# Top-k attention and a hard-swish feed-forward part: query tiles outermost, 128-token blocks, V as stationary operand, mask on GpSimd

## The chip, the cores and the metric

One core of a Trainium2 chip runs the kernel. Its engines run side by side, each with a queue of its own that it takes in order: TensorE (PE; its weight loads are shown as PEld), VectorE (DVE), ScalarE (ACT), GpSimd (POOL), and SyncE (SP), which here only issues DMAs. The metric is the device time of one execution in microseconds, less is better.

## The reference

Everything is float32, except that the two weight matrices arrive as float64.

```python
# q, k, v: (8 batches, 8 heads, 576 rows, 64)
scores = (q @ k.transpose(0, 1, 3, 2)) / 8
kth = 32nd largest score of each row
scores = where(scores >= kth, scores, -1e9); scores -= max
attn = exp(scores); attn /= attn.sum(-1) + 1e-9
x = (attn @ v), heads side by side          # (4608 tokens, 512)
h = x @ w_in                                # 512 -> 2048
out = (h * clip(h + 3, 0, 6) / 6) @ w_out   # 2048 -> 512
```

## The kernel before

The work is cut into 160 **units**. A pair of heads of one batch has five: four full ones (128 queries of each of the two heads, so two tiles of 128x576 scores) and one "rest" unit (the 64 queries left over of both heads in one tile). Pairs are outermost: all five units of a pair, then the next pair; 20 units make a batch.

For a unit TensorE makes the scores (line 201, contraction over 64 features, the two heads in the two halves of the array's rows), ScalarE copies them to SBUF (L203), and VectorE finds the 32nd largest of each row in four rounds of "eight largest" (L215) and "replace them" (L218). ScalarE takes the exponential (L223, its shift from GpSimd, L221), and VectorE sets to 0 what is below the 32nd largest (L227). TensorE then transposes the weights in blocks of 128x128 (L243, L251), ScalarE copies them back (L244, L252), and ten products per unit give the weighted values (L259): there the transposed weights are the stationary operand, 128x128, and V with a column of ones moves, 65 columns. VectorE divides by the sum (L267 to L270), and one more transpose (L277, copied at L280) puts features on partitions.

The feed-forward part runs over blocks of 512 tokens, one per batch, and one for the left-over rows of all batches. A block has 16 times four products of 512 moving columns (L289), each group followed by a ScalarE relu (L297) and a VectorE gate (L299), then four times 16 products of 512 columns (L307). The program deals a batch's block out in pieces of four products among the units of the next batch; the last batch's block and that of the left-over rows come at the end. Every matrix product in float32 is two instructions in the trace (1152 for 576 products at L307); a transpose is one.

The float64 weights are converted in 64 chunks of 128x256 during the first batch (L101 to L123: a DMA, six VectorE and two GpSimd operations each), through 16 shared buffers. The tile framework's scheduler sets the order on each engine.

Of the kernel before, what the change touches and what calls it, by code (L numbers as in the profile page):

```python
# [15 lines left out]
LOWEST = -3.4028234663852886e38  # L16
EPS = 1.0e-9
# High words of the float64 values that float32 can hold, read as float32: 0x38000000 and
# 0x47efffff. Below the first they become 0.
# [5 lines left out]
def kernel(  # L25
# [16 lines left out]
    NC = J + 1  # L42
    NHP = H // 2
    NFC = FF // P
    TB = JP  # tokens in a block of the feed-forward part
    DE = D + 1
    assert 2 * D == P and 2 * R == P and NHP * P == DM
    assert TB == 512 and DM == 512 and B * R == TB and TOP_K % 8 == 0
# [7 lines left out]
    kqpool = pool("kq", 2)  # L56
    scpool = pool("sc", 3)
    wkpool = pool("wk", 4)
    mpool = pool("m", 3)
    epool = pool("e", 2)  # L60
    etpool = pool("et", 2)
    xpool = pool("x", 2)
    xtpool = pool("xt", 2)
    gpool = pool("g", NFC)
    tpool = pool("t", 2)
    opool = pool("o", 2)
    ps_sc = pool("ps_sc", 1, space=PSUM)
    ps_w = pool("ps_w", 3, space=PSUM)
    ps_acc = pool("ps_acc", 1, space=PSUM)
# [3 lines left out]

    def work():
        return ps_w.tile([P, 512], F32, tag="w", name="w")
# [5 lines left out]
    # A last column of ones gives the sum of the weights next to the weighted values. The last  # L81
    # tile of keys is the last 128 of them: its first half is another tile's, and counts for 0.
    NV = 3
    vring = []
    for i in range(NV):
        t = const([P, 2, NC, DE], f"v{i}")
        nc.gpsimd.memset(t[:], 1.0)
        nc.gpsimd.memset(t[0 : P - R, :, J, :], 0.0)
        vring.append(t)
    w_in = const([P, NHP, FF], "w_in")  # L90
    w_out = const([P, NFC, DM], "w_out")
    x_rest = const([P, NHP, TB], "x_rest")  # left-over rows of all batches: a block of their own

# [1 line left out]

    WC = 256

    def convert(dst, src):
        """dst[P, WC] = src[P, WC], rounded once; src holds float64 bits, low word first."""
        st = gpool.tile([P, 2 * WC], U32, tag="g", name="st")  # L100
# [3 lines left out]
        ta = gpool.tile([P, 2, WC], F32, tag="g", name="ta")  # L104
        sp = gpool.tile([P, 2, WC], F32, tag="g", name="sp")
        t, a, s, p = ta[:, 0, :], ta[:, 1, :], sp[:, 0, :], sp[:, 1, :]
        tu, au, su = t.bitcast(U32), a.bitcast(U32), s.bitcast(U32)
        nc.vector.tensor_scalar(tu, hi, 0x7FFFFFFF, None, ALU.bitwise_and)
        nc.gpsimd.tensor_scalar(t, t, HI_MOST, HI_LEAST, ALU.min, ALU.max)
        # The exponent's top bit stays, the three after it go; the rest moves up by three.  # L110
        nc.vector.tensor_scalar(
            au, tu, 3, 0x3FFFFFFF, ALU.logical_shift_left, ALU.bitwise_and
        )
        nc.vector.scalar_tensor_tensor(
            out=au, in0=tu, scalar=0x40000000, in1=au, op0=ALU.bitwise_and, op1=ALU.bitwise_or
        )
        # The low word counts in units of 2**-52 of the power of two.
        nc.vector.tensor_scalar(su, au, 0x7F800000, None, ALU.bitwise_and)
        nc.vector.scalar_tensor_tensor(
            out=p, in0=lo, scalar=2.0**-52, in1=s, op0=ALU.mult, op1=ALU.mult  # L120
        )
        nc.gpsimd.tensor_tensor(a, a, p, ALU.add)
        nc.vector.scalar_tensor_tensor(  # L123
            out=dst.bitcast(U32), in0=hi, scalar=0x80000000, in1=au,
            op0=ALU.bitwise_and, op1=ALU.bitwise_or,
        )

    def weight_chunks():
        win, wout = moe_w_in.bitcast(U32), moe_w_out.bitcast(U32)
        for f in range(0, FF, WC):  # L130
            for g in range(NHP):
                rows = slice(g * P, (g + 1) * P)
                yield w_in[:, g, f : f + WC], win[rows, 2 * f : 2 * (f + WC)]
        for c in range(NFC):
            for e in range(0, DM, WC):
                rows = slice(c * P, (c + 1) * P)
                yield w_out[:, c, e : e + WC], wout[rows, 2 * e : 2 * (e + WC)]

# [1 line left out]

    class Pair:
        """Two heads of a batch: their loads, and keys and queries with the head dim on partitions."""

        def __init__(self, i):
            self.b, self.hp = divmod(i, NHP)
            self.v = vring[i % NV]

        def load(self):
            h0 = 2 * self.hp
            for name, src in (("kin", k), ("qin", q)):  # L150
                t = ldpool.tile([P, NC, 2, D], F32, tag=name, name=name)
# [9 lines left out]
            for hh in range(2):  # L161
                nc.sync.dma_start(
                    self.v[:, hh, 0:J, 0:D],
                    v[self.b, h0 + hh, 0:JP, :].rearrange("(p j) d -> p j d", j=J),
                )
            nc.sync.dma_start(
                self.v[P - R : P, :, J, 0:D], v[self.b, h0 : h0 + 2, JP:S, :].rearrange("h s d -> s h d")
            )

        def transpose(self):  # L170
            kT = self.kT = kqpool.tile([P, S], F32, tag="kT", name="kT")
            qT = self.qT = kqpool.tile([P, S], F32, tag="qT", name="qT")
            for src, dst in ((self.kin, kT), (self.qin, qT)):
                ps = work()
# [3 lines left out]
                nc.scalar.copy(dst[:, 0:JP], ps[:, 0:JP])  # L178
            ps = work()
# [3 lines left out]
            for i, dst in enumerate((kT, qT)):  # L183
                nc.scalar.copy(dst[:, JP:S], ps[:, i * R : (i + 1) * R])

    class Unit:
        """A tile of queries: 128 of each head of a pair, or the 64 left over of both in one."""
# [6 lines left out]
        def scores(self):  # L194
            pr, nt, q0 = self.pair, self.nt, self.qt * P
            ps = ps_sc.tile([P, 2, 1024], F32, tag="ps", name="ps")
            for s0, s1 in ((0, 512), (512, S)):
                for hh in range(2):
                    d = slice(hh * D, (hh + 1) * D)
                    dst = ps[hh * R : (hh + 1) * R, 0, s0:s1] if self.rest else ps[:, hh, s0:s1]  # L200
                    nc.tensor.matmul(dst, pr.qT[d, q0 : min(q0 + P, S)], pr.kT[d, s0:s1])  # L201
            self.sc = scpool.tile([P, 2, S], F32, tag="sc", name="sc")
            nc.scalar.copy(self.sc[:, 0:nt, :], ps[:, 0:nt, 0:S])  # L203

        def weights(self):
            """exp(scale * (s - max)) where s reaches the row's TOP_K-th largest score, else 0."""
            nt, sc = self.nt, self.sc
            m = mpool.tile([P, 2, TOP_K], F32, tag="m", name="m")
            shift = mpool.tile([P, 2], F32, tag="shift", name="shift")
            e = self.e = epool.tile([P, 2, S], F32, tag="e", name="e")  # L210
            cur = [sc[:, t, :] for t in range(nt)]
            for r in range(TOP_K // 8):
                for t in range(nt):
                    m8 = m[:, t, 8 * r : 8 * r + 8]
                    nc.vector.max(m8, cur[t])  # L215
                    if r < TOP_K // 8 - 1:
                        wk = wkpool.tile([P, S], F32, tag="wk", name="wk")
                        nc.vector.match_replace(wk[:], m8, cur[t], LOWEST)  # L218
                        cur[t] = wk[:]
                if r == 0:  # L220
                    nc.gpsimd.tensor_scalar_mul(shift[:, 0:nt], m[:, 0:nt, 0], -scale)  # L221
                    for t in range(nt):
                        nc.scalar.activation(  # L223
                            e[:, t, :], sc[:, t, :], AF.Exp, bias=shift[:, t : t + 1], scale=scale
                        )
            for t in range(nt):
                nc.vector.scalar_tensor_tensor(  # L227
                    out=e[:, t, :],
                    in0=sc[:, t, :],
                    scalar=m[:, t, TOP_K - 1 : TOP_K],  # L230
                    in1=e[:, t, :],
                    op0=ALU.is_ge,
                    op1=ALU.mult,
                )

        def values(self, dst):
            """Weighted values over the sum of the weights, with features on partitions, to dst."""
            pr, nt, e = self.pair, self.nt, self.e
# [182 lines left out]
```

## Time and profile before

| | us |
|---|---|
| median of three runs | 2309.13 (2308.7 to 2310.08) |
| span of the profiled execution, first to last instruction | 2307.1 |
| TensorE matmuls busy | 2060.9 (89%) |
| VectorE busy | 1874.4 (81%) |
| ScalarE busy | 760.6 (33%) |
| GpSimd busy | 120.0 (5%) |

The span is that of one execution; the runs' time lies 2.0 us above it. A busy share is a mean over the span, in which three stretches differ: the first batch with the weights' conversion up to some 440 us, the seven batches up to 2076 us, and the last two feed-forward blocks. The clock that TensorE was granted is one of two levels, 1.2 and 2.4 GHz; the windows' column gives its mean as a share of 2.4 GHz.

### The profile page before, as it was taken

What the parts mean: (1) busy time and instruction counts of PE and PEld (TensorE: products, weight loads), DVE (VectorE), ACT (ScalarE), POOL (GpSimd) and SP (SyncE); (2) the same over time, 40 slices, a digit from 0 to 9 for tenths busy, and PEclk for the clock granted to TensorE, in tenths of its full rate; (3) what the DMA queues carried; (4) which work ended last, traced back from release to release, by engine and by line L of the source; (5) the groups of instructions that cost most, each with busy time, mean ns of one, the idle gap of its engine ahead of it and who ended that gap; (6) DMA issues with size and microseconds to landing.
All of it is one profiled execution on the core that took longest, in us unless ns stands there. A gap on an engine that the chain in (4) does not pass through costs nothing.

```text
span 2307.1 us, 25080 instructions
## 1 busy us (share of the span) xinstructions
PE 2060.9 (89%) x8704; PEld 1170.3 (51%) x8704; DVE 1874.4 (81%) x4177; ACT 760.6 (33%) x1365; POOL 120.0 (5%) x300
## 2 busy tenths in 40 slices
PE   7566662799999999999899989998999999999998
PEld 4444441456555655555455545565555555654443
DVE  7999988689998998989898989988998989881010
ACT  3222220234343433433334333333334333431020
POOL 1222212000000000000000000000000000000000
PEclk9765556799999998999999999999999999999999
DMA  3021211000100000000000100000001000000000
GB/s 98 28 75 42 71 42 46 11 16 22 29 16 16 25 25 16 16 21 25 21 8 22 32 11 16 19 23 25 16 11 31 25 11 6 10 10 0 14 5 18
DMA packets 129790, 56.15 MB, mean 24 GB/s; under 512 B 116864, under 2 KB 116864, under 8 KB 129664
## 3 DMA queue, kind: packets, MB, share of 16 engines
q1 hardware_dynamic: 129664, 54.55, 8.8%
q8 instruction: 69, 1.13, 0.2%
q14 instruction: 57, 0.47, 0.1%
HBM read 45.09 MB, written 9.44 MB: 24 GB/s over the span
## 4 chain that ended last, share of the span: by engine, by line
PE 72%; DVE 7%; ACT 2%; issue 1%; DVEq 0%; POOL 0%; ACTq 0%
PE w L289 22%; PE acc L307 20%; PE w L259 12%; PE ps L201 10%; PE w L251 5%; DVE m L215 3%; DVE wk L218 2%; PE w L243 1%; PE w L277 1%; DVE e L227 1%; ACT sc L203 1%; PE w L177 1%; PE w L182 0%; DVE x L270 0%; DVE den L267 0%
## 5 line engine op out<-in xcount | busy, mean ns | idle before, releaser
L215 DVE MAX8 m<-wk 128x8 f32<-128x576 f32 x864 | 624.3, 747 | 0.8
L307 PE MATMUL acc<-w_out,g 128*128 128x512 f32 x1152 | 548.4, 607 | 2.1 <-ACT o L317 2.1
L201 PE MATMUL ps<-kT,qT 64*128 64x64 f32 (+3 forms) x1280 | 399.0, 501 | 113.2 <-ACT sc L203 113.0
L289 PE MATMUL w<-xT,w_in 128*128 128x512 f32 x1024 | 476.7, 619 | 0.0
L259 PEld LDWEIGHTS w<-v,eT 128*128 128x128 f32 (+1 forms) x3200 | 374.8, 195 | 104.8 <-ACT eT L252 55.3
L218 DVE MATCH_REPLACE8 wk<-m,wk 128x576 f32<-128x576 f32 x576 | 425.3, 741 | 0.3 <-issue 0.3
L259 PE MATMUL w<-v,eT 128*128 128x65 f32 (+1 forms) x3200 | 390.7, 279 | 3.4 <-ACT eT L252 3.3
L203 ACT COPY sc<-ps 128x1152 f32<-128x1152 f32 (+1 forms) x160 | 163.7, 1023 | 481.8 <-PE ps L201 259.4
L289 PEld LDWEIGHTS w<-xT,w_in 128*128 128x128 f32 x1024 | 200.1, 201 | 228.6 <-issue 227.1
L307 PEld LDWEIGHTS acc<-w_out,g 128*128 128x128 f32 x1152 | 200.7, 190 | 181.0 <-issue 165.3
L201 PEld LDWEIGHTS ps<-kT,qT 64*128 64x128 f32 (+1 forms) x1280 | 144.2, 192 | 262.1 <-ACT sc L203 149.3
L223 ACT ACTIVATE e<-sc,shift 128x576 f32<-128x576 f32 x288 | 214.2, 776 | 130.4 <-POOL shift L221 130.0
L297 ACT ACTIVATE t<-w,three 128x512 f32<-128x512 f32 x144 | 99.0, 687 | 474.2 <-PE w L289 417.4
L299 DVE SCALAR_TENSOR_TENSOR g<-t,w 128x512 f32<-128x512 f32 x144 | 97.9, 680 | 191.7 <-ACT t L297 191.6
L227 DVE SCALAR_TENSOR_TENSOR e<-sc,m,e 128x576 f32<-128x576 f32 x288 | 228.0, 807 | 8.6 <-ACT e L223 8.2
L215 DVE MAX8 m<-sc 128x8 f32<-128x576 f32 x288 | 212.2, 745 | 18.1 <-ACT sc L203 17.7
L218 DVE MATCH_REPLACE8 wk<-m,sc 128x576 f32<-128x576 f32 x288 | 212.8, 740 | 0.0
L251 PE MATMUL w<-ident,e 128*128 128x128 f32 x1152 | 179.6, 294 | 2.2 <-ACT xT L280 0.7
L252 ACT COPY eT<-w 128x512 f32<-128x512 f32 x288 | 162.6, 591 | 46.0 <-PE w L251 41.6
L251 PEld LDWEIGHTS w<-ident,e 128*128 128x128 f32 x1152 | 144.2, 152 | 34.2 <-ACT eT L252 21.2
L221 POOL TENSOR_SCALAR shift<-m 128x2 f32<-128x2 f32 (+1 forms) x160 | 38.2, 239 | 1662.0 <-DVE m L215 1095.0
L267 DVE TENSOR_SCALAR den<-w 128x2 f32<-128x2 f32 (+1 forms) x160 | 24.6, 154 | 120.4 <-PE w L259 120.3
(45 smaller groups left out, 885.1 us busy)
## 6 DMA issues: line engine op xcount, KB each, us to landing
kin<-in_k_dram SPq DMA_DIRECT2D x64, 128.0 KB, 2.7
qin<-in_q_dram SPq DMA_DIRECT2D x64, 128.0 KB, 2.9
v<-in_v_dram SPq DMA_DIRECT2D x64, 128.0 KB, 2.7
st<-in_moe_w_in_dram SPq DMA_DIRECT2D x32, 256.0 KB, 3.7
st<-in_moe_w_out_dram SPq DMA_DIRECT2D x32, 256.0 KB, 3.3
out_dram<-o SPq DMA_DIRECT2D x32, 256.0 KB, 2.3
kin<-in_k_dram SPq DMA_DIRECT2D x32, 32.0 KB, 2.4
qin<-in_q_dram SPq DMA_DIRECT2D x32, 32.0 KB, 2.5
```

Of the source, the lines that this page charges most:

```text
L201: nc.tensor.matmul(dst, pr.qT[d, q0 : min(q0 + P, S)], pr.kT[d, s0:s1])
L203: nc.scalar.copy(self.sc[:, 0:nt, :], ps[:, 0:nt, 0:S])
L215: nc.vector.max(m8, cur[t])
L218: nc.vector.match_replace(wk[:], m8, cur[t], LOWEST)
L223: nc.scalar.activation(e[:, t, :], sc[:, t, :], AF.Exp, bias=shift[:, t : t + 1], scale=scale)
L227: nc.vector.scalar_tensor_tensor(out=e[:, t, :], in0=sc[:, t, :], scalar=m[:, t, TOP_K - 1 : TOP_K], in1=e[:, t, :], op0=ALU.is_ge, op1=AL ...
L251: nc.tensor.transpose(ps[:, cs], e[:, t, cs], ident[:])
L252: nc.scalar.copy(eT[:, t, 0:J, :], ps[:, 0:JP].rearrange("p (c q) -> p c q", c=J))
L259: nc.tensor.matmul(o[:, hh, :], eT[:, t, c, q0 : q0 + ql], pr.v[:, hh, c, :], start=(c == 0), stop=(c == J),)
L289: nc.tensor.matmul(h[:], w_in[:, i, f * P : (f + 1) * P], xT[:, i, :], start=(i == 0), stop=(i == NHP - 1),)
L297: nc.scalar.activation(t[:], h[:], AF.Relu, bias=three[:], scale=1.0)
L307: nc.tensor.matmul(acc[:], gs[f][:, ts * P : (ts + 1) * P], w_out[:, f, :], start=(f == 0), stop=(f == NFC - 1),)
```

## The change

Within a batch the query tile is now the outer loop and the four pairs the inner one: four units (one tile of 128 queries, all eight heads) complete a block of 128 tokens, whose feed-forward part can follow at once. There are 36 such blocks: four per batch, and one for the left-over rows of every two batches. A block is eight pieces: four of 16 products with 128 moving columns (four chunks of the hidden layer in one PSUM bank, one relu and one gate on 128x512 for all four), and four of four products with 512 moving columns. In the values' products V is the stationary operand (64 columns; the output of one head goes to partitions 0 to 63, of the other to 64 to 127) and the transposed weights move, 128 columns. The scores of both heads lie side by side; the last 64 keys of both heads are one product over all 128 rows.

The mask is made on GpSimd (compare and multiply by -3e38, add to the scores, both before the exponential); the exponential gives the sum of the weights, and ScalarE multiplies the weights by its reciprocal before they are transposed. The transpose of x and the division on VectorE are gone. Weights are converted in 32 chunks of 128x512 through two load buffers, with other operations. The order on each engine is now the order of the code. Cut to its core (the new kernel's lines):

```diff
+    scpool = pool("sc", 4)
+    stpool = pool("st", 2)
+    cvpool = pool("cv", 2)
+    opool = pool("o", 1)
     ps_sc = pool("ps_sc", 1, space=PSUM)
+    ps_tr = pool("ps_tr", 2, space=PSUM)
+    ps_w = pool("ps_w", 2, space=PSUM)
+    ctx.enter_context(tc.manual_schedule())
...
         nc.sync.dma_start(st[:], src)
...
+        nc.scalar.activation(f, lo, AF.Copy, scale=2.0**-52)
+        nc.scalar.activation(a, hi.bitcast(F32), AF.Abs)
+        nc.gpsimd.tensor_scalar(a, a, HI_MOST, HI_LEAST, ALU.min, ALU.max)
...
+        nc.vector.tensor_scalar(au, au, 0x40000000, None, ALU.bitwise_xor)
+        nc.gpsimd.tensor_tensor(f, f, s, ALU.mult)
+        nc.gpsimd.tensor_tensor(a, a, f, ALU.add)
...
+                nc.tensor.matmul(ps[:, 0:JP], pr.qT[h0, qs], pr.kT[h0, :])
+                nc.tensor.matmul(ps[:, S + R : 1024], pr.qT[h1, qs], pr.kT[h1, 0 : 1024 - S - R])
+                nc.tensor.matmul(ps[:, 1024:W2], pr.qT[h1, qs], pr.kT[h1, 1024 - S - R : JP])
+                nc.tensor.matmul(ps[:, JP : S + R], pr.qT[:, qs], pr.kr[:].rearrange("p h r -> p (h r)"))
+                nc.scalar.copy(sc[:], ps[:, 0:W2])
...
+                nc.gpsimd.tensor_scalar(
+                    self.wk[:, t, :], self.row[t], self.m[:, t, TOP_K - 1 : TOP_K], DROP,
+                    ALU.is_lt, ALU.mult,
+                )
...
+                nc.scalar.activation(
+                    self.row[t], self.row[t], AF.Copy, scale=self.den[:, t : t + 1]
+                )
...
+                    nc.tensor.matmul(
+                        dst[hh * D : (hh + 1) * D, :],
+                        pr.vm[:, hh, c, :] if c < J else pr.vr[:, hh, :],
+                        rhs,
...
+            g = gpool.tile([P, 512], F32, tag="g", name="g")
+            nc.scalar.activation(g[:], h[:], AF.Relu, bias=three[:], scale=1.0)
...
+        if u:
+            u.begin()
+            u.top(0)
+        run_gate()
+        if n >= FF_FROM:
+            piece()
+        if u:
+            u.top(1)
+        if 2 <= n < NU + 2:
+            units[n - 2].weights()
...
+        if u:
+            u.top(2)
+        run_gate()
+        if n >= FF_FROM and (two or n % 4 == 3):
+            piece()
...
+        if n >= 2 and n < NU + 2 and (n - 2) % 2 == 1:
+            values(n - 2)
+        if u:
+            u.top(3)
+        if chunks:
+            convert_some(3)
+        if n >= FF_FROM and two and n % 4 == 3:
+            run_gate()
+            piece()
+        if u:
+            u.mask()
+        if 1 <= n < NU + 1:
+            units[n - 1].exp()
```

In iteration n VectorE thus works on unit n (`top`: one round for both heads; four rounds), TensorE makes the scores of unit n + 1, and the transposes are those of unit n - 2; the values of two units follow in every second iteration. `weights` is the multiplication by the reciprocal. The order of three places follows.

On ScalarE, in the middle of the program, this stood for one unit before (the scores' copy, a copy of x, a relu, the copies of the transposed weights, an exponential):

```order
L203 COPY sc<-ps 128x1152
L280 COPY xT<-w 128x128
L297 ACTIVATE t<-w,three 128x512
L244 COPY eT<-w 128x2x128
L252 COPY eT<-w 128x512 x2
L223 ACTIVATE e<-sc,shift 128x576
```

and this stands for one iteration with two first-half pieces now (L221 copies the scores, L329 is a relu, L270 multiplies by the reciprocal, L284 copies the transposed weights, L259 is the exponential):

```order
L221 COPY sc<-ps 128x1152
L329 ACTIVATE g<-h,three 128x512
L270 ACTIVATE sc<-sc,den 128x576 x2
L284 COPY eT<-tr 128x512 x2
L329 ACTIVATE g<-h,three 128x512
L259 ACTIVATE sc,den<-sc,shift 128x576 x2
```

So the two multiplications, on which the transposes of that unit rest, now stand behind the relu of the piece that TensorE runs just ahead of those transposes.

On TensorE the same iteration reads now (scores of the next unit, first piece, transposes, second piece):

```order
L217 MATMUL ps<-kT,qT 128x512
L218 MATMUL ps<-kT,qT 128x384
L219 MATMUL ps<-kT,qT 128x128
L220 MATMUL ps<-kr_157,qT 128x128
L321 MATMUL h<-xT,w_in 128x128 x16
L282 MATMUL tr<-ident,sc 128x128 x4
L291 MATMUL rt<-ident,sc 128x128
L282 MATMUL tr<-ident,sc 128x128 x4
L321 MATMUL h<-xT,w_in 128x128 x16
```

where before, in the second batch, pieces (L289) stood among products of several units, and the scores of a unit (L201) were split among them:

```order
L289 MATMUL w<-xT,w_in 128x512 x4
L243 MATMUL w<-ident,e 128x128 x2
L251 MATMUL w<-ident,e 128x128 x4
L201 MATMUL ps<-kT,qT 64x512
L201 MATMUL ps<-kT,qT 64x64 x2
L251 MATMUL w<-ident,e 128x128 x4
L259 MATMUL w<-v_113,eT 128x65 x10
L277 MATMUL w<-ident,x 128x128
L289 MATMUL w<-xT,w_in 128x512 x8
```

The first piece now stands directly ahead of the transposes, and the scores' products of a unit stand together.

On VectorE, in the first batch, the operations of a conversion stood singly among the rounds of a unit before (L108 to L123 are the conversion's):

```order
L215 MAX m<-wk 128x8
L118 TENSOR_SCALAR sp<-ta 128x256
L218 MATCH_REPLACE wk<-m,wk 128x576
L119 SCALAR_TENSOR_TENSOR sp<-st,sp 128x256
L215 MAX m<-wk 128x8
L123 SCALAR_TENSOR_TENSOR w_in<-st,ta 128x256
```

and now three chunks follow in one run behind a unit's last round (L114 to L120 are three operations of one chunk, L125 finishes the chunk before it):

```order
L232 MAX m<-wk 128x8 x2
L114 TENSOR_SCALAR cv<-cv 128x512
L117 TENSOR_SCALAR cv<-cv 128x512
L120 TENSOR_SCALAR cv<-cv 128x512
L114 TENSOR_SCALAR cv<-cv 128x512
L117 TENSOR_SCALAR cv<-cv 128x512
L120 TENSOR_SCALAR cv<-cv 128x512
L125 SCALAR_TENSOR_TENSOR w_in<-st,cv 128x512
```

Nothing of a unit stands between the chunks any more.

## Rows read from the trace of the kernel before

**Rows 1.** The page: engines (busy us, share, instructions), and the chain's shares.
```profile
PE 2060.9 (89%) x8704; PEld 1170.3 (51%) x8704; DVE 1874.4 (81%) x4177; ACT 760.6 (33%) x1365; POOL 120.0 (5%) x300
...
PE 72%; DVE 7%; ACT 2%; issue 1%; DVEq 0%; POOL 0%; ACTq 0%
```

**Rows 2.** Windows: length, busy us (instructions) by engine, clock, DMA share, GB/s.
```profile
120.00:230.00 110.00, 72.54 (x274) 48.38 (x273) 102.76 (x265) 27.14 (x49) 23.74 (x42) 0.56 0.20 60
...
461.40:2076.40 1615.00, 1551.83 (x7128) 887.72 (x7126) 1456.37 (x3148) 621.96 (x1127) 32.21 (x133) 0.98 0.07 19
488.95:731.00 242.05, 238.07 (x1114) 136.95 (x1114) 220.81 (x473) 98.13 (x180) 5.25 (x20) 0.99 0.09 22
2076.40:2307.10 230.70, 223.99 (x513) 97.81 (x513) 22.07 (x33) 26.97 (x41) 0.00 (x0) 0.99 0.03 9
```

**Rows 3.** Timeline of TensorE at full clock: start, us, instructions merged.
```profile
639.84 0.27 PE L251 MATMUL w<-ident,e 128*128 128x128 f32 x1
...
641.58 1.23 PE L259 MATMUL w<-v,eT 128*128 128x65 f32 x10
642.74 1.12 PE L201 MATMUL ps<-kT,qT 64*128 64x512 f32 x2
643.79 1.33 PE L259 MATMUL w<-v,eT 128*128 128x65 f32 x10
...
646.71 1.19 PE L201 MATMUL ps<-kT,qT 64*64 64x512 f32 x8 [0.16 <-ACT sc L203]
...
648.00 7.03 PE L289 MATMUL w<-xT,w_in 128*128 128x512 f32 x16
...
657.24 1.04 PE L251 MATMUL w<-ident,e 128*128 128x128 f32 x8
...
659.25 2.45 PE L259 MATMUL w<-v,eT 128*128 128x65 f32 x20
```

**Rows 4.** Timeline of TensorE in the first unit, at half clock.
```profile
8.37 2.40 PE L201 MATMUL ps<-kT,qT 64*128 64x512 f32 x8 [0.27 <-ACT qT L178]
```

**Rows 5.** Timeline of VectorE in the first unit.
```profile
11.96 1.42 DVE L215 MAX8 m<-sc 128x8 f32<-128x576 f32 x2 [11.10 <-ACT sc L203]
...
21.62 1.53 DVE L227 SCALAR_TENSOR_TENSOR e<-sc,m,e 128x576 f32<-128x576 f32 x2
```

**Rows 6.** Groups by line and form: busy us, mean ns, idle before.
```profile
L227 DVE SCALAR_TENSOR_TENSOR e<-sc,m,e 128x576 f32<-128x576 f32 x288 | 228.0, 807 | 8.6 <-ACT e L223 8.2
L223 ACT ACTIVATE e<-sc,shift 128x576 f32<-128x576 f32 x288 | 214.2, 776 | 130.4 <-POOL shift L221 130.0
...
L307 PEld LDWEIGHTS acc<-w_out,g 128*128 128x128 f32 x1152 | 200.7, 190 | 181.0 <-issue 165.3 <-ACT o L317 6.6 <-DVE den L267 1.2
...
L252 ACT COPY eT<-w 128x512 f32<-128x512 f32 x288 | 162.6, 591 | 46.0 <-PE w L251 41.6
...
L297 ACT ACTIVATE t<-w,three 128x512 f32<-128x512 f32 x144 | 99.0, 687 | 474.2 <-PE w L289 417.4 <-DVE g L299 54.5 <-PE w L243 2.3
L299 DVE SCALAR_TENSOR_TENSOR g<-t,w 128x512 f32<-128x512 f32 x144 | 97.9, 680 | 191.7 <-ACT t L297 191.6
...
L122 POOL TENSOR_TENSOR ta<-ta,sp 128x256 f32<-128x256 f32 x64 | 49.9, 780 | 174.0 <-DVE sp L119 149.7 <-DVE den L267 13.7 <-DVE den L268 10.5
...
L109 POOL TENSOR_SCALAR ta<-ta 128x256 f32<-128x256 f32 x64 | 29.0, 454 | 106.2 <-issue 62.0 <-DVE ta L108 20.5 <-DVE den L268 14.4
...
L111 DVE TENSOR_SCALAR ta<-ta 128x256 uint32<-128x256 uint32 x64 | 18.3, 286 | 6.6 <-POOL ta L109 6.6
...
L123 DVE SCALAR_TENSOR_TENSOR w_in<-st,ta 128x256 uint32<-128x256 uint32 x32 | 13.6, 426 | 6.2 <-POOL ta L122 5.0
```

**Rows 7.** DMA issues by line: KB each, median us to landing.
```profile
v<-in_v_dram SPq DMA_DIRECT2D x64, 128.0 KB, 2.7
st<-in_moe_w_in_dram SPq DMA_DIRECT2D x32, 256.0 KB, 3.7
st<-in_moe_w_out_dram SPq DMA_DIRECT2D x32, 256.0 KB, 3.3
```

**Rows 8.** Timeline of the DMA queue: issue of the first two loads.
```profile
0.72 1.36 SPq L154 DMA_DIRECT2D kin<-in_k_dram  x2
```

More of the change, by code (lines that the diff above doesn't have):

```diff
@@ L203, in scores @@
[L203 to L234, printed above, removed]
@@ new lines, in transpose, with blocks @@
+        def transpose(self, rt):
+            sc = self.sc
+            eT = self.eT = etpool.tile([P, 2 * J, P], F32, tag="eT", name="eT")
+            def blocks(dst, starts):
+                ps = ps_tr.tile([P, 512], F32, tag="tr", name="tr")
+                for i, c0 in enumerate(starts):
+                    nc.tensor.transpose(ps[:, i * P : (i + 1) * P], sc[:, c0 : c0 + P], ident[:])
+                n = len(starts) * P
+                nc.scalar.copy(dst.rearrange("p c q -> p (c q)"), ps[:, 0:n])
+            main = [c * P for c in range(J)]
+            blocks(eT[:, 0:J, :], main)
+            if self.rest:
+                blocks(eT[:, J : J + 2, :], [JP, S - P])
+            else:
+                nc.tensor.transpose(rt, sc[:, JP : JP + P], ident[:])
+                blocks(eT[:, J : 2 * J, :], [S + R + c0 for c0 in main])
@@ L322, in rows_of_batch @@
-    def rows_of_batch(b):
-        return lambda ts: [(0, P, out[b * S + ts : b * S + JP : J, :])]
-    def rows_left(ts):
-        return [
-            (i * R, (i + 1) * R, out[(2 * ts + i) * S + JP : (2 * ts + i + 1) * S, :])
-            for i in range(2)
-        ]
-    NP = B * NHP
-    pairs = [Pair(i) for i in range(NP)]
-    units = [Unit(pr, qt) for pr in pairs for qt in range(NC)]
-    per_batch = NHP * NC
-    pieces = 2 * NFC
-    chunks = list(weight_chunks())
-    per_step = -(-len(chunks) // (per_batch - 2))
@@ new lines, with piece @@
+    pairs = {(b, hp): Pair(b, hp) for b in range(B) for hp in range(NHP)}
+    units = []
+    for b in range(B):
+        tiles = list(range(J))
+        tiles = tiles + [J] if b % 2 == 0 else [J] + tiles
+        for qt in tiles:
+            units += [Unit(pairs[b, hp], qt) for hp in range(NHP)]
+    per_batch = NHP * (J + 1)
+    NU = len(units)
+    todo = []
+    gate = None
+    def piece():
+        nonlocal gate
+        while todo:
+            try:
+                gate = next(todo[0])
+                return
+            except StopIteration:
+                todo.pop(0)
@@ new lines, in run_gate, with convert_some @@
+    def run_gate():
+        nonlocal gate
+        if gate:
+            gate()
+        gate = None
+    chunks = [(dst, src) for dst, src in weight_chunks()]
+    finishes = []
+    def convert_some(n):
+        for dst, src in chunks[:n]:
+            finishes.append(convert(dst, src))
+            if len(finishes) > 1:
+                finishes.pop(0)()
+        del chunks[:n]
+        if not chunks:
+            while finishes:
+                finishes.pop(0)()
+    FF_FROM = 8
+    state = {}
@@ L390 @@
+    while todo:
+        run_gate()
+        piece()
 _INS = ["q", "k", "v", "moe_w_in", "moe_w_out"]
```

391 lines of the change are left out of this document (203 added, 188 removed).

## The prediction

> **What bounds the kernel now.** I read the page first, then windows, then TensorE's timeline. TensorE is busy for 2060.9 us of 2307.1 and carries 72% of the chain that ended last, VectorE 7% [rows 1]. The windows show that this is three kernels in one. In the first batch TensorE has little to do (72.5 us of 110, at clock 0.56) while VectorE is busy for 102.8: the weights' conversion sets the pace. In the middle TensorE is busy for 1551.8 of 1615 us at clock 0.98, VectorE for 1456.4; a batch takes 242. At the end VectorE is all but idle for 230.7 us while two feed-forward blocks run alone [rows 2]. So what counts is TensorE's price per unit, what keeps it waiting in its own queue, and the two ends.
>
> **Prices on TensorE, full clock.** A product of 128 columns that loads its own 128x128 weights comes every 0.11 us: eight transposes take 1.04, the last of them 0.27, so 0.77/7. The old values' products, 65 columns with such weights, come no faster: (2.45 - 0.27)/19 = 0.115. Sixteen products of 512 columns take 7.03, the last 0.59: 0.43 each [rows 3]. I take 0.112 for 128 columns (bounds 0.110 and 0.115). Products in different halves of the rows run at once: the eight scores' instructions of a full unit take 2.40 at half clock, where one after the other they would need 4 x 0.86 + 4 x 0.11 = 3.9; a rest unit's eight take 1.19 at full clock, not 1.95 [rows 4, 3]. A change of tile shape costs some 0.2: from 642.74 to 643.79 pass 1.05 us for two products of 0.43 [rows 3].
>
> **The change, part by part.** *Removed:* VectorE's mask, 288 x 0.807 = 228 us [rows 6], with the division and x's transpose. This is worth nothing by itself where TensorE is the bound. Also removed is the lone end: the last block now has 128 tokens.
>
> *Feed-forward products.* 36 blocks of four pieces of 32 instructions at 0.112 (3.58 us) and four pieces of eight at 0.43 (3.44). Six pieces run before unit 11, the other 140 and 142 make 140 x 3.58 + 142 x 3.44 = 989 us. Cutting the moving side from 512 to 128 columns costs only 0.005 per product.
>
> *Attention's products.* Full unit: scores 2 x 0.43 with the heads at once (they now stand together) + 0.22 for the product over all rows, 2.5 changes of shape 0.5, nine transposes 0.99, values 20 x 0.11. The last is the unknown. The two heads' values lie in different column halves over the same rows, and no row of before shows that form. From below, they pair as the row halves do: 1.1 us per unit; from above, they do not: 2.2. The nearest rows, the rest unit's scores, differ in rows and columns at once and start together, so I take 1.1. The Trainium skill's TensorEngine Tiling (Array Packing), When to Use Tiling, names this very swap (a moving side of 64 or less becomes stationary, with two column tiles); no run here shows it yet. The unit is 3.67 us; 117 units from the eleventh on make 429. A rest unit is 1.07 + 0.5 + 0.66 + 0.57 = 2.8, x 32 = 90. Transposing keys and queries: 26 x 1.4 = 36. Sum 555.
>
> *A new wait.* ScalarE takes its queue in order, and the two multiplications of unit n - 2 stand behind the relu of the piece just ahead of that unit's transposes. When the piece's last column is through, TensorE waits for its latency (0.16), the relu (0.69), the first multiplication (0.78, as the exponential's 128x576) and hand-overs of some 0.05 each, runs four transposes (0.44) while the second comes, 0.67 later, and waits again: 1.87 us in all [rows 3, 6]. Queued behind on TensorE are the second piece, the values and the next scores; on VectorE the gates. The pattern repeats every four units: pieces one and three, and the last one with its scaling of the result, stand in that place, so three waits a block: 35 x 3 x 1.87 = 196. Where keys are transposed too (26 times), their copies delay each other by some 0.85; and the values wait some 0.2 for the last block's copy: 32 together.
>
> *What is hidden.* GpSimd's mask is 2 x 0.75 + 2.76 + 0.22 = 4.5 us by the slopes of L109 and L122 (0.93 and 2.2 ns an element over 0.22) [rows 6]; the next unit's first two rounds, 5.6, cover it. Beyond that each us goes onto VectorE's path. VectorE needs 9.66 per full unit (21.62 - 11.96) [rows 5] and 0.68 for each gate [rows 6]: four units 42.5, against TensorE's 4 x 3.67 + 28.1 + 6.5 of waits + 1.5 = 51. So it has cover, and waits at the gates. ScalarE's added multiplications are 1.5 us per unit and hidden but for the wait above. Where there are no pieces (two units in each odd batch) VectorE sets the pace: 15. The clock of 0.98 in the middle [rows 2] means 4% at half, 32 us lost; I keep these 32.
>
> *The opening.* Before the first load of weights 40 loads go through the queue, 0.66 each [rows 8]: 27 us. Then three chunks stand behind each unit's rounds, with two load buffers: the second and the third chunk can only be loaded when the chunk two before is finished, so VectorE stands still for a load, two ScalarE copies (1.2) and a GpSimd operation (0.69). 128 KB land in 2.7 us and 256 KB in 3.3 to 3.7 [rows 7]; 512 KB then need 3.5 to 5.1, I take 4.2. With hand-overs that is 6.4, twice a unit. The VectorE work is 9.66 + 3 x 1.5 + 3 x 0.73 (three operations of 0.45 and hand-overs, and the finish, scaled from L111 and L123 [rows 6]) = 16.4. A unit: 29.2. Unit 0 ends at 49; nine more make 263; the last, with two chunks, 27. In units 2 to 9 ScalarE comes late to its copies, behind transposes and values at half clock and at the end behind pieces: 2 us in even units, 7 to 10 in odd ones, 51 together (bounds 20 and 90). Sum 390.
>
> *The end.* After the last product its latency, the scaling of the result and the store: 7.
>
> **Sum.** 390 + 989 + 555 + 228 + 15 + 32 + 7 = 2216 against the span of 2307; the runs lie 2 us above their span, so 2218, 4% less. Check on the old middle: a batch's block of 256 products at 0.43 (110), 16 units of 2.2 + 1.2 + 1.8 + 1.6, four of 3.2, pairs 5: 237, against 238.1 busy of 242.
>
> **Rivals.**
> *The values do not pair* (other side). The two column halves take turns: 117 x 1.1 + 32 x 0.57 = 147, and 18 more in the opening, where they run at half clock: 2383. For it speaks that no row shows two streams over the same rows; against it the rows' pairs [rows 3, 4]. It decides alone from 100 us on, that is, if some three fifths of the pairing fail.
> *The relu's wait is covered.* If TensorE gets its weights earlier than ScalarE's queue suggests, the 196 vanish, and so may part of the opening's 51: about 2030. Against it stands the order of the queue.
> *The clock falls in every cycle.* In the first batch, where TensorE pauses often, it has 0.56 [rows 2]. If the last piece, with the values and the waits after it, were enough in each of 36 cycles, at some 4 us each: 2360. Against it: 0.99 in a batch before with its pauses.
> *Weight loads show.* One load lasts 0.19 (L307, PEld) [rows 6]. If each of 4608 products of 128 columns waited for its own instead of 0.112: 359 more, 2577. The transposes at 0.11 with a load each speak against it. The Trainium skill's TensorE: Matmul & The Clock Gate, Back-to-back issue gap, has 81 ns sustained against 56 alone at 128 columns, a ratio of 1.45; as an estimate from that page the pieces would cost some 230 us more. By that rule this change would end slower; the rows, at 0.115 against 0.107 for the columns alone, do not show it.
>
> **Numbers.** Chances: the forecast 0.50 (own range 2120 to 2320), no pairing 0.20, wait covered 0.15, clock 0.10, weight loads 0.05. The range is 2050 to 2400: it leaves out half of "wait covered" below, and the weight loads with the upper part of "no pairing" above. Faster by more than 0.2% (about what a measurement of this kernel can tell from no change): nearly all of the forecast, all of "wait covered", a little of the two next: 0.68; within it 0.03; slower 0.29.
>
> **What would show it.** Right: conversions until about 390 us, with VectorE idle before L114, released by GpSimd; then cycles of four full units of some 51 us; TensorE idle before L282, released by L270, for about 1.9 us three times a cycle; values' starts in pairs a few ns apart; 128-column products every 0.112 us; VectorE idle at L333. Wrong: values spaced 0.11 without pairs; a clock under 0.95 in the middle; idle time of VectorE behind GpSimd's mask; an opening far from 390 either way, which is the term with the least support.

## The result and the profile after

The changed kernel takes 2210.72 us (median of four runs, 2209.28 to 2212.43) against 2309.27 before: a ratio of 0.9574, 95% interval 0.956 to 0.9587. The forecast was 2218. The profiled execution has a span of 2207.5.

The page of the changed kernel, engines and chain, which answer to [rows 1]:

```profile
PE 1697.8 (77%) x11904; PEld 1227.9 (56%) x11904; DVE 1612.1 (73%) x3313; ACT 999.7 (45%) x1893; POOL 1216.6 (55%) x918
...
PE 64%; DVE 10%; POOL 9%; issue 8%; ACT 4%; DMA 4%; SPq 0%; ACTq 0%; POOLq 0%
```

TensorE is less busy, and GpSimd, which did next to nothing, is busy for 55%. The windows (columns as in [rows 2]) are those of the opening from the second unit to the last conversion, of the middle, of one place where rest units follow each other, and of the end:

```profile
49.20:414.30 365.10, 79.03 (x490) 61.42 (x488) 186.41 (x331) 91.44 (x166) 183.53 (x138) 0.69 0.15 47
580.00:1000.00 420.00, 380.61 (x2730) 277.61 (x2726) 339.90 (x715) 218.08 (x416) 247.44 (x176) 1.00 0.08 21
1500.00:1550.00 50.00, 39.24 (x295) 31.44 (x294) 42.87 (x93) 22.85 (x45) 30.02 (x20) 0.90 0.17 42
2151.70:2207.50 55.80, 50.83 (x301) 33.52 (x299) 3.77 (x8) 14.03 (x27) 7.15 (x6) 1.00 0.03 10
```

In the opening no engine is busy for more than 51%: it is bound by waits. In the middle TensorE works at full clock for 91%, with VectorE at 81%. The end is 56 us where it was 231.

Where the 99 us came from is seen by cutting both traces at every 144th of VectorE's 1152 operations "eight largest" (one batch's worth). The first batch lasts 508 us (304 before), the second 236 (304), the other six 233 each (242), and from the last of these operations to the end of the work it is 53 us (233). So the opening lost 204, the second batch gave back 68, the middle gave 54, and 180 came from the end, where two feed-forward blocks of 512 tokens no longer run alone. What the order of the query tiles, the smaller blocks and V as the stationary operand each gave of the 54 was not separated: of the change's parts only the comparison on GpSimd was undone by itself (below).

TensorE's timeline of the changed kernel in the middle (start, us, merged instructions):

```profile
700.54 3.74 PE L321 MATMUL h<-xT,w_in 128*128 128x128 f32 x32
704.12 0.60 PE L180 MATMUL kq<-ident,kin 128*128 128x128 f32 x4
...
705.80 1.09 PE L304 MATMUL pv<-eT,vm 128*64 128x128 f32 x16
706.88 0.44 PE L304 MATMUL pv<-rT,vr 128*64 128x128 f32 x4
707.15 1.04 PE L304 MATMUL pv<-eT,vm 128*64 128x128 f32 x16
708.02 0.39 PE L304 MATMUL pv<-rT,vr 128*64 128x128 f32 x4
708.34 3.70 PE L340 MATMUL acc<-w_out,g 128*128 128x512 f32 x8
711.97 0.69 PE L217 MATMUL ps<-kT,qT 64*128 64x512 f32 x1
...
713.36 3.60 PE L340 MATMUL acc<-w_out,g 128*128 128x512 f32 x8
716.80 0.60 PE L282 MATMUL tr<-ident,sc 128*128 128x128 f32 x4
...
717.78 3.60 PE L340 MATMUL acc<-w_out,g 128*128 128x512 f32 x8
...
732.88 3.74 PE L321 MATMUL h<-xT,w_in 128*128 128x128 f32 x32
738.11 0.63 PE L282 MATMUL tr<-ident,sc 128*128 128x128 f32 x4 [1.49 <-issue]
...
738.89 0.60 PE L282 MATMUL tr<-ident,sc 128*128 128x128 f32 x4
```

The values of two units (40 instructions, those with the left-over keys included) take 2.54 us from start to start (705.80 to 708.34), so the heads run at once: their starts come in pairs 0.007 apart (705.797 and 705.804), one pair every 0.11. In the same way a first-half piece of 32 instructions takes 3.58, one of eight 3.44 (713.36 to 716.80), the scores 1.39, nine transposes 0.98. And ahead of the L282 at 738.11 stands the wait that was forecast, but put down to "issue", that is, to nothing the profile shows. ScalarE's timeline at the same place tells what it is:

```profile
736.65 0.69 ACT L329 ACTIVATE g<-h,three 128x512 f32<-128x512 f32 x1 [2.15 <-PE h L321]
737.24 1.43 ACT L270 ACTIVATE sc<-sc,den 128x576 f32<-128x576 f32 x2
```

The relu runs, then the two multiplications behind it, and at 738.0 the first of them is done: 0.1 us later TensorE goes on. Against a queue without waits it loses 738.11 - 732.88 - 3.58 = 1.65, and 0.24 more between its two groups of transposes.

The groups by line (busy, mean ns, idle before) with what was not as forecast:

```profile
L246 POOL TENSOR_SCALAR wk<-sc,m 128x576 f32<-128x576 f32 x288 | 636.4, 2218 | 613.2 <-DVE m L232 613.2
L251 POOL TENSOR_TENSOR sc<-sc,wk 128x1152 f32<-128x1152 f32 x128 | 337.1, 2633 | 10.7
L111 POOL TENSOR_SCALAR cv<-cv 128x512 f32<-128x512 f32 x32 | 19.6, 612 | 180.0 <-ACT cv L110 179.9
L125 DVE SCALAR_TENSOR_TENSOR w_in<-st,cv 128x512 uint32<-128x512 uint32 x16 | 28.0, 1752 | 0.0
L268 DVE RECIPROCAL den<-den 128x2 f32<-128x2 f32 x128 | 20.7, 162 | 154.4 <-POOL den L264 154.4
L114 DVE TENSOR_SCALAR cv<-cv 128x512 uint32<-128x512 uint32 x32 | 13.6, 426 | 166.7 <-POOL cv L111 166.7
```

VectorE's waits up to 420 us (us in total, times, longest), the line for L268:

```profile
DVE den L268 <- POOL den L264: 28.7, 9, 3.3
```

The comparison on GpSimd (L246) takes 2.22 us, not 0.75, and L125 1.75, not 0.73. VectorE waits for GpSimd at L268 (the reciprocal, behind the addition of 1e-9 at L264), where no wait was forecast; idle time of VectorE behind the mask was one of the prediction's own signs of being wrong.

### The profile page after: what moved, and what is told of

Its sections match the earlier page's. It is cut to its first block, busy times and chain, and to the rows that moved or that the text cites. A ratio compares the mean times of both kernels' runs of the same rounds, so it can differ in the third digit from the quotient of the medians.

```text
span 2207.5 us, 31292 instructions
## 1 busy us (share of the span) xinstructions
PE 1697.8 (77%) x11904; PEld 1227.9 (56%) x11904; DVE 1612.1 (73%) x3313; ACT 999.7 (45%) x1893; POOL 1216.6 (55%) x918
## 4 chain that ended last, share of the span: by engine, by line
PE 64%; DVE 10%; POOL 9%; issue 8%; ACT 4%; DMA 4%; SPq 0%; ACTq 0%; POOLq 0%
PE h L321 21%; PE acc L340 19%; PE pv L304 7%; PE tr L282 7%; POOL sc L251 4%; POOL wk L246 3%; DVE m L232 3%; PE ps L217 3%; DVE wk L236 3%; PE ps L220 2%; DMA st<-in_moe_w_out_dram 2%; DMA st<-in_moe_w_in_dram 2%; PE ps L218 1%; PE rt L291 1%; DVE w_in L125 1%
## 5 line engine op out<-in xcount | busy, mean ns | idle before, releaser
L246 POOL TENSOR_SCALAR wk<-sc,m 128x576 f32<-128x576 f32 x288 | 636.4, 2218 | 613.2 <-DVE m L232 613.2
L282 PE MATMUL tr<-ident,sc 128*128 128x128 f32 x1216 | 195.2, 290 | 467.5 <-issue 390.0
L321 PE MATMUL h<-xT,w_in 128*128 128x128 f32 x4096 | 481.5, 276 | 0.0
L321 PEld LDWEIGHTS h<-xT,w_in 128*128 128x128 f32 x4096 | 469.2, 193 | 1.6 <-issue 0.5
L282 PEld LDWEIGHTS tr<-ident,sc 128*128 128x128 f32 x1216 | 147.0, 148 | 533.2 <-issue 472.6
L251 POOL TENSOR_TENSOR sc<-sc,wk 128x1152 f32<-128x1152 f32 (+1 forms) x160 | 382.1, 2388 | 13.3
L329 ACT ACTIVATE g<-h,three 128x512 f32<-128x512 f32 x144 | 98.9, 687 | 371.6 <-PE h L321 371.6
L270 ACT ACTIVATE sc<-sc,den 128x576 f32<-128x576 f32 x288 | 208.1, 766 | 129.9 <-DVE den L268 129.8
L333 DVE SCALAR_TENSOR_TENSOR g<-g,h 128x512 f32<-128x512 f32 x144 | 98.5, 684 | 194.6 <-ACT g L329 194.6
L284 ACT COPY eT<-tr 128x512 f32<-128x512 f32 x320 | 176.5, 566 | 110.0 <-PE tr L282 101.2
L259 ACT ACTIVATE sc<-sc,shift 128x576 f32<-128x576 f32 x288 | 220.8, 770 | 0.0
L221 ACT COPY sc<-ps 128x1152 f32<-128x1152 f32 x128 | 142.1, 1110 | 159.4 <-PE ps L220 158.4
L268 DVE RECIPROCAL den<-den 128x2 f32<-128x2 f32 (+1 forms) x160 | 26.0, 162 | 195.6 <-POOL den L264 195.4
L304 PE MATMUL pv<-eT,vm 128*64 128x128 f32 (+1 forms) x2560 | 161.0, 270 | 0.0
L217 PE MATMUL ps<-kT,qT 64*128 64x512 f32 x256 | 151.7, 674 | 0.8 <-ACT qT L181 0.8
```

The costliest lines, as they stand in the source:

```text
L217: nc.tensor.matmul(ps[:, 0:JP], pr.qT[h0, qs], pr.kT[h0, :])
L246: nc.gpsimd.tensor_scalar(self.wk[:, t, :], self.row[t], self.m[:, t, TOP_K - 1 : TOP_K], DROP, ALU.is_lt, ALU.mult,)
L251: nc.gpsimd.tensor_tensor(both, both, self.wk[:, 0:nt, :].rearrange("p t s -> p (t s)"), ALU.add)
L259: nc.scalar.activation(self.row[t], self.row[t], AF.Exp, bias=self.shift[:, t : t + 1], scale=scale, accum_out=self.den[:, t : t + 1],)
L270: nc.scalar.activation(self.row[t], self.row[t], AF.Copy, scale=self.den[:, t : t + 1])
L282: nc.tensor.transpose(ps[:, i * P : (i + 1) * P], sc[:, c0 : c0 + P], ident[:])
```

## The experiments

All are edits of the changed kernel (2211 us), or of it with the earlier edits that are named.

**The two heads' values, one after the other.**
```diff
-            for c in range(J + 1):
-                for hh in range(2):
+            for hh in range(2):
+                for c in range(J + 1):
```


> The changed kernel with one edit: the values' products of one head all stand ahead of those of the other, where the two heads alternated. Theory (the heads' products run at once, in two halves of the columns): a full unit's 20 products, 1.2 to 1.35 us in the changed kernel's trace, take 20 x 0.112 = 2.24, so 1.0 more for each of 117 full units from the eleventh on and 0.5 for 32 rest units, +130, near 2340 us (2320 to 2360). Rival (starts a few ns apart are only how the records are written, and each product has its turn of 0.056 anyway): within 5 us of 2211.

Measured: 2292.4 us, 82 more, which refutes the rival but falls short of the range. Its timeline of TensorE, first and last rows of the values of two units and what follows:
```profile
724.66 1.09 PE L304 MATMUL pv<-eT,vm 128*64 128x128 f32 x8
725.74 0.32 PE L304 MATMUL pv<-rT,vr 128*64 128x128 f32 x1
...
728.09 0.38 PE L304 MATMUL pv<-rT,vr 128*64 128x128 f32 x2
728.40 3.70 PE L340 MATMUL acc<-w_out,g 128*128 128x512 f32 x8
```
The 40 instructions take 3.74 us in place of 2.54. The first ones start every 0.11 alone; but where one head's run ends and the next head's begins, starts again come in pairs (725.737 and 725.744, 726.449 and 726.455). One after the other at 0.112 they would take 4.48 (an estimate), so the edit undid some three fifths of the pairing, 1.20 of 1.94 us. Pairing is shown: 0.6 us a full unit for this part; the price of none at all was not measured.

**The 1e-9 on VectorE.**
```diff
-            nc.gpsimd.tensor_scalar_add(d, d, EPS)
...
+            nc.vector.tensor_scalar_add(d, d, EPS)
             nc.vector.reciprocal(d, d)
```


> The changed kernel with one edit: the 1e-9 is added to the sum of the weights on VectorE, ahead of the reciprocal, and not on GpSimd, where the addition stands behind the next unit's mask of 7.3 us. Theory (the mask is longer than predicted, but in the middle VectorE's wait for it is hidden behind TensorE's wait for the relu): only the waits of the opening go, 8 of 3.3, so -25 to -30: 2180 to 2188 us. Rival (VectorE's wait for GpSimd, 125.7 us after the opening, is on the path there too): -80 or more, 2130 or less.

Measured: 2175.4 us, 35 less, 5 beyond the range. The last conversion ends at 394.0 (414.3 before the edit), so 20 of the 35 lie in the opening. Blocks in the middle, from the last product of one to that of the next, take 50.28 and 48.72 us as before the edit; only at three places where rest units stand did a block get some 3 us shorter (57.2 for 60.65) and its neighbour 1. So the wait for GpSimd is hidden in the middle, as theory had it, and costs in the opening and a little at the rest units.

**The multiplications ahead of the relu, too.**
```diff
             u.top(0)
+        if 2 <= n < NU + 2:
+            units[n - 2].weights()
         run_gate()
...
-            units[n - 2].weights()
             d = units[n - 2]
```


> As the kernel with the 1e-9 on VectorE, and the reciprocal and ScalarE's two multiplications of unit n - 2 stand ahead of the piece and its relu, not behind it. Theory (TensorE waits 1.65 + 0.24 us, three times in each of 35 blocks, for the relu and the two multiplications behind it in ScalarE's queue): these 198 us go, TensorE's four units need 43.1 (44.6 with the transposes of keys), VectorE's 43.4, and where the two engines wait for each other at the gates some 1 to 2 a block come back: 130 to 180 less than the kernel with the 1e-9 on VectorE, 2005 to 2055. Rival (TensorE waits there for something else, as the trace names no releaser for most of these waits): less than 30 us gained. Second rival (VectorE, waiting for the relu at its gates, becomes the bound at once): some 60 gained.

Measured: 2001.1 us, 174 less than with the 1e-9 alone and just under the range. In its timeline the transposes follow the piece at once:
```profile
746.30 3.74 PE L320 MATMUL h<-xT,w_in 128*128 128x128 f32 x32
749.87 0.60 PE L281 MATMUL tr<-ident,sc 128*128 128x128 f32 x4
...
750.42 0.60 PE L281 MATMUL tr<-ident,sc 128*128 128x128 f32 x4
```
and a window of its middle has TensorE busy for 98%:
```profile
455.00:905.00 450.00, 441.96 (x3216) 324.13 (x3215) 420.07 (x879) 247.45 (x482) 277.10 (x174) 1.00 0.10 25
```
So the wait called "issue" was ScalarE's queue. 23 of the 174 lie in the opening (its last conversion ends at 371.0, not 394.0), so 151 of the 198 came back; what kept the other 47 was not taken apart. TensorE is the limit in this window, and VectorE, now busy for 93%, is close behind it.

**The same without the 1e-9.** The edit above alone.

> The changed kernel with the reciprocal and the multiplications ahead of the relu, but the 1e-9 left on GpSimd, behind the next unit's mask. Theory (VectorE then waits for GpSimd's queue one round earlier, with 2.8 us of cover in place of 5.6 for a mask of 7.5): VectorE stands still for 4.7 us in each unit, four units take 4 x (9.66 + 0.16 + 4.7) + 2.7 = 61 and not 50, and the gain of 174 turns into a loss of 250 to 370, 2460 to 2580 us. Rival (the relu was the only thing waited for): near the 2001 of the kernel with both.

Measured: 2501.2 us, 290 more. VectorE's and GpSimd's timelines in the middle:
```profile
704.05 0.17 DVE L268 RECIPROCAL den<-den 128x2 f32<-128x2 f32 x1 [3.57 <-POOL den L264]
```
```profile
700.76 2.62 POOL L251 TENSOR_TENSOR sc<-sc,wk 128x1152 f32<-128x1152 f32 x1
...
703.79 0.22 POOL L264 TENSOR_SCALAR den<-den 128x2 f32<-128x2 f32 x1
```
The one small addition waits for the next unit's whole mask, and everything on VectorE behind it: blocks of 58.8 us for 50.3. The GpSimd mask that the prediction called hidden is hidden only by the round that stands ahead of L268; take that away and it costs more than the relu did.

**L125 first.**
```diff
+            if finishes:
+                finishes.pop(0)()
             finishes.append(convert(dst, src))
-            if len(finishes) > 1:
-                finishes.pop(0)()
```


> The changed kernel with one edit: the last operation of the conversion of a chunk (L125) stands ahead of the next chunk's conversion, not behind its three VectorE operations. Theory (with two load buffers the next load starts only when L125 has run, so load, ScalarE, GpSimd and VectorE follow each other for every chunk, 8.8 us, and L125, which then runs beside GpSimd's multiplication, takes 1.75 in place of 0.69): the next load now goes out while VectorE works on the chunk before, three chunks behind a unit take 13 to 15 us and not 21 to 24, and 60 to 90 us go: 2120 to 2150. Rival (the load itself sets the pace): the stalls of 5.8 stay and at most the 34 us of the longer L125 go.

Measured: 2136.8 us, 74 less; the last conversion ends at 342.8. VectorE's wait at L114 falls from 166.7 to 58.5, and L125 itself to 0.69 (median). Half of what L114 gave back returns as a wait ahead of L125, which now follows its chunk's last GpSimd operation (L122) at once: 54.9 us in all, where it was 1.2. What the edit did not take away is L268's wait, now 4.67 in seven of nine units.

**Chunks spread over the rounds, too.**
```diff
+        if chunks:
+            convert_some(1)
         if u:
             u.top(2)
...
+        if chunks:
+            convert_some(1)
         if u:
             u.top(3)
         if chunks:
-            convert_some(3)
+            convert_some(1)
```


> As the kernel with L125 first, and the three chunks stand singly behind the second, third and last round of a unit. Theory (in the opening VectorE waits for one chunk's chain because three chunks stand in one run): each chain of load, ScalarE and GpSimd gets 2.8 us of rounds beside it, and the pace of a unit falls from 29.7 to that of GpSimd, 3 x 3.7 + 7.7 = 18.8, or a little more; ten units: 60 to 100 less than the kernel with L125 first, 2040 to 2080 us. Rival (ScalarE and TensorE come late in the opening at half clock, and set the pace): less than 30 gained.

Measured: 2119.2 us, only 18 less: a miss. VectorE, GpSimd and ScalarE in one unit of the opening:
```profile
197.72 0.43 DVE L114 TENSOR_SCALAR cv<-cv 128x512 uint32<-128x512 uint32 x1 [4.93 <-POOL cv L111]
```
```profile
184.27 4.41 POOL L246 TENSOR_SCALAR wk<-sc,m 128x576 f32<-128x576 f32 x2
188.76 2.61 POOL L251 TENSOR_TENSOR sc<-sc,wk 128x1152 f32<-128x1152 f32 x1
...
191.78 0.22 POOL L264 TENSOR_SCALAR den<-den 128x2 f32<-128x2 f32 x1
197.07 0.61 POOL L111 TENSOR_SCALAR cv<-cv 128x512 f32<-128x512 f32 x1 [5.08 <-ACT cv L110]
```
```profile
192.23 1.44 ACT L270 ACTIVATE sc<-sc,den 128x576 f32<-128x576 f32 x2 [9.99 <-DVE den L268]
...
195.78 0.67 ACT L109 ACTIVATE cv<-st 128x512 f32<-128x512 uint32 x1
196.34 0.65 ACT L110 ACTIVATE cv<-st 128x512 f32<-128x512 f32 x1
```
The rival was right that ScalarE comes late, and the trace shows what makes it late: the mask (GpSimd, until 191.5) holds the 1e-9, that the reciprocal, that the multiplications, transposes and their copies, and the chunk's two copies (L109, L110) stand behind those on ScalarE.

**All four edits.**

> The 1e-9 on VectorE, the multiplications ahead of the relu, L125 first and the chunks spread, all together. If opening and middle are apart, as theory has it, the gains add: 174 for the multiplications, some 10 to 35 for the 1e-9 and that of the spread kernel: 1850 to 1900 us, four units at 44.7 to 46.5 and conversions over by about 260 us. Rival (with the opening faster TensorE's queue fills where it waited before, and part is given back): 1920 or more.

Measured: 1906.7 us, a ratio to the kernel before of 0.8266 (0.8252 to 0.828). The gains add (2211 - 35 - 174 - 92 = 1910), as theory had it; the range was missed by 7 us, because it still counted on what spreading had not brought.

**GpSimd's comparison in two other forms.**
```diff
-                nc.gpsimd.tensor_scalar(
-                    self.wk[:, t, :], self.row[t], self.m[:, t, TOP_K - 1 : TOP_K], DROP,
-                    ALU.is_lt, ALU.mult,
-                )
+                if t == 0:
+                    nc.gpsimd.tensor_scalar(
+                        self.wk[:, t, :], self.row[t], 0.5, DROP, ALU.is_lt, ALU.mult
+                    )
+                else:
+                    nc.gpsimd.tensor_scalar(
+                        self.wk[:, t, :], self.row[t], self.m[:, t, TOP_K - 1 : TOP_K], 0.0,
+                        ALU.min, ALU.max,
+                    )
```


> The changed kernel with GpSimd's comparison in two other forms, so the mask is not the reference's: for the first tile of a unit the same two operations (less than, multiply) with a constant in place of the row's own 32nd value, for the second other operations (minimum, maximum) with the row's own value. Theory (a value per row is what makes it 2.22 us, against 0.61 for 512 elements in L111, which has two constants): the first tile's falls to about 0.69, the second's stays at 2.2. Rival (the comparison is slow, whatever the operand): the first stays at 2.2 and the second falls to 0.7. Second rival (something beside it on VectorE slows it): both stay.

Measured: 2182.5 us in one run, 28 less. The kernel leaves the right mask out, so only the prices of the two forms are read from it. Groups of GpSimd (L247 is the first form, L251 the second):
```profile
L247 POOL TENSOR_SCALAR wk<-sc 128x576 f32<-128x576 f32 x160 | 344.0, 2150 | 656.2 <-DVE m L232 655.3
L251 POOL TENSOR_SCALAR wk<-sc,m 128x576 f32<-128x576 f32 x128 | 94.9, 741 | 12.0
```
The rival was right: the operations set the price, not the operand.

**Without a comparison.** On the kernel with all four edits:
```diff
-                    self.wk[:, t, :], self.row[t], self.m[:, t, TOP_K - 1 : TOP_K], DROP,
-                    ALU.is_lt, ALU.mult,
-                )
+                    self.wk[:, t, :], self.row[t], self.m[:, t, TOP_K - 1 : TOP_K], 0.0,
+                    ALU.subtract, ALU.min,
+                )
+            drop = self.wk[:, 0:nt, :].rearrange("p t s -> p (t s)")
+            nc.gpsimd.tensor_scalar_mul(drop, drop, 1e30)
```


> As the kernel with all four edits, and GpSimd makes the mask without a comparison: subtract the row's 32nd value and take the minimum with 0 (0.74 each, as the minimum and maximum with a value per row were), times 1e30 for both tiles (1.3), then the addition as before. Theory (the comparison alone is slow on GpSimd): the mask falls from 7.3 to 5.6 us, a unit of the opening by that, and the middle not at all, since TensorE is the bound there: 12 to 20 less, 1887 to 1895 us. Rival (the subtraction costs 2.2 as well): no gain or some 10 more.

Measured: 1922.2 us, 15 more: a miss, and the rival was right. The mask's operations in its groups:
```profile
L246 POOL TENSOR_SCALAR wk<-sc,m 128x576 f32<-128x576 f32 x288 | 635.5, 2215 | 142.1 <-DVE m L232 133.0 <-ACT g L330 7.6 <-ACT kT L181 1.1
L251 POOL TENSOR_SCALAR wk<-wk 128x1152 f32<-128x1152 f32 x128 | 401.9, 3140 | 11.2
```
Subtract with minimum costs as much as the comparison, and one multiplication 2.7 ns an element; of the forms run here only minimum with maximum is quick (1.2 to 1.3 ns). The opening got 31 us longer, the rest 16 shorter, though the mask is 3 us longer: why the middle gained is open.

**The comparison on VectorE.**
```diff
-                nc.gpsimd.tensor_scalar(
+                nc.vector.tensor_scalar(
```


> The changed kernel with one part undone: the comparison of the mask goes back to VectorE, the addition stays on GpSimd. GpSimd's mask falls from 7.3 to 2.9 us, VectorE gets two operations of 0.48 to 0.75 a unit. Theory (GpSimd's mask costs only the 3.3 us per unit in the opening, and VectorE has 7 us of cover in four units of the middle): -29 and + 10 x 1.2 in the opening, nothing in the middle: 2190 to 2200 us. Rival (moving the mask to GpSimd is where the change won time): slower, by up to 36 x 4 x 1.2 = 170, 2380.

Measured: 2186.0 us, 25 less, 4 beyond the range. VectorE's operation takes 0.545 on average:
```profile
L246 DVE TENSOR_SCALAR wk<-sc,m 128x576 f32<-128x576 f32 x288 | 146.3, 545 | 1.1
```
Moving the comparison off VectorE gained nothing; it cost these 25.

**The comparison on VectorE in the opening alone,** on the kernel with all four edits:
```diff
-                nc.gpsimd.tensor_scalar(
+                compare.tensor_scalar(
...
-            u.mask()
+            u.mask(nc.vector if n < 11 else nc.gpsimd)
```


> As the kernel with all four edits, and the mask's comparison stands on VectorE in the first eleven units, as long as weights are converted, and on GpSimd behind them. Theory (in the opening GpSimd's queue sets the pace: a chunk's first GpSimd operation stands behind the mask of 7.3 us): GpSimd's need per unit falls from 18.5 to 14, VectorE's rises to 17.3, and a unit of the opening falls from 22.8 to 18: 35 to 50 less, 1857 to 1872 us. Rival (the loads or ScalarE set the pace there): within 10 of 1907.

Measured: 1913.5 us, 7 more: a miss. VectorE's waits at L114 fall from 73.8 to 52.4 us, but its 22 comparisons take 30.5:
```profile
L246 DVE TENSOR_SCALAR wk<-sc,m 128x576 f32<-128x576 f32 x22 | 30.5, 1426 | 0.0
```
The mean is 1.43: the 20 that begin beside GpSimd's two-tile operations on a chunk (L121, L122) take 1.51 to 1.52 each, the two others 0.50 and 0.52. The same shows in the run before, where ten of 288 took 1.51, all of them behind an L122, and the rest 0.50 to 0.52. The waits that are left end with ScalarE's copies, as the rival had it.

## Why the prediction was right, and where not

The time came within 7 us, and in part by luck: two errors, of some 24 and 33 us, cancelled in it. The mechanisms of the middle were right.

**The opening: 390 forecast, 414.3 measured.** From the second unit on it is 365.1 for 341. The shape was right: VectorE stands still twice a unit for a serial chain of load, copies and GpSimd. Nineteen such stalls are 5.87 each (forecast 6.4), and those before a unit's first chunk 35.4 in all (51): 26 less. *The step that failed* is the cover of GpSimd's mask, "4.5 us", which "the next unit's first two rounds, 5.6, cover": the mask is 7.3, and in nine units of the opening VectorE waits 28.7 for it at L268. Its slope came from an operation with minimum and maximum (L109 [rows 6]), which the last experiments show to be the only quick pair of those run. Mis-sized besides is L125, 1.75 for 0.73: some 30 more in all. That is 33 more for 24 measured; the 9 between were not taken apart.

**After the opening: 1826 forecast, 1793 measured.** The pieces are 3.58 and 3.44 as put in. A full unit's attention products are 1.39 (scores, to the next start) + 0.98 + 1.27 (values) = 3.64, for 3.67: the values cost 0.17 more, the rest less. The relu's wait is 1.65 + 0.24 = 1.89, for 1.87, and taking it away gave back 151 of its 198. (The terms that the prediction names for it add up to more, some 1.96 with two hand-overs; what it used without saying so is that ScalarE's next operation starts 0.1 before the record of the one before ends, 737.24 against 736.65 + 0.69. VectorE's four units, put at 42.5, are 41.4 by the two terms named, 4 x 9.66 + 4 x 0.68; nothing hung on that.) Too dear were the keys' transposes and the clock. A block with transposes is 50.28 - 48.73 = 1.55 longer, for 2.25 (18 us over 26). After 414.3 the clock is at half for 43 us in all, which can cost 22 at most, for 32; 31 of the 43 lie at the three later places where rest units follow each other, as in the window with 0.90 above. These two are 28 of the 33; the units that VectorE paces, 15, could not be told from the clock.

**The rivals.** No pairing: the starts in pairs refute it, and undoing some three fifths of it costs 82 us. The relu covered: it was not, but the order of two calls, with the 1e-9 moved, makes it so, at 2001 us for the 2030 that the rival gave (2218 less its 196 is 2022). The clock falling in each cycle: 1.00 over 420 us of the middle, though TensorE idles three times a block. Weight loads: the products come every 0.112 us as the rows of before had it, and not 1.45 times as slowly, as by the ratio from the Trainium skill's TensorE: Matmul & The Clock Gate, Back-to-back issue gap.

## What to carry to other kernels

When an operation moves to another engine, price it there by a row with the same operations, not the same shape: one slope, from minimum with maximum, stood for a form three times as dear. A wait that costs nothing has a cover; know which instructions it is made of before moving any of them, since the same reordering gave 174 us where one small addition had been moved first, and cost 290 where it had not. And where the trace names "issue" ahead of an instruction with several inputs, look at the end of each producer on its own engine.

## What the hardware showed

GpSimd's operation with two constants or a value per row takes 0.61 to 0.74 us for 512 to 576 elements with minimum and maximum, and 2.15 to 2.22 for 576 with less-than and multiply or with subtract and minimum.

VectorE's L125, with two inputs in SBUF, takes 1.75 us in 31 of 32 cases beside GpSimd's multiplication of two tiles (L121), 0.69 in the one without, and a median of 0.69 where it is moved (1.09 in the six cases that begin beside L111). At 210.18 it starts 0.29 after GpSimd's, which ends at 211.39, and ends at 211.93, 0.54 behind that. The Trainium skill's SBUF — State Buffer, Who interferes with whom, says that a VectorE instruction with two SBUF inputs contends with a GpSimd one that reads SBUF, and that the later one is held up wholly; these ends agree with that. The gates (L333), whose second input is in PSUM, take 0.67 to 0.69 at any time, also the 18 that begin beside the mask's addition (L251). But two whole tiles in SBUF are not needed for it: VectorE's comparison, which has one tile and a value per row, took 1.51 in place of 0.51 when it began beside L121 or L122. In the run with all comparisons on VectorE the first of these ends 0.31 behind L122 (GpSimd until 50.62, VectorE until 50.93).

TensorE does not take its queue strictly in order, as the opening section has it of every engine. With the heads apart, the next head's first product started, by the trace, at 725.744, after the first and before the second of the two instructions (725.737 and 725.897) of the last product of the head before, which stands ahead of it in the code. The two go to different column halves.
